# A fused attention and gated MoE kernel on one core: weight steps moved to VectorE, two chunks in turn, a rearranged start

## The chip, the cores and the metric

The kernel runs on one core of one Trainium2 chip. The metric is the device time of one execution in microseconds (us); lower is better. Engines are TensorE (PE; its weight loads PEld), VectorE (DVE), ScalarE (ACT), GpSimd (POOL) and SyncE (SP, which here only issues transfers; ScalarE issues some too). TensorE's clock has two levels, 1.2 and 2.4 GHz; the profile gives the granted clock as a fraction of the higher one.

## What is computed

```python
# attention: q, k, v are [4, 8, 576, 64]; hidden layer of 32
scores = matmul(q, k^T) / sqrt(64)
x      = log1p(|i - j|) / log1p(max(i, 1))             # [576, 576]
scores = scores + (relu(x * w1 + b1) @ w2) per head     # the position bias
attn   = softmax(scores) ;  y = attn @ v                # -> 2304 tokens x 512
# gated MoE layer: 512 -> 1536 -> 512
out = (sigmoid(y @ w_gate) * (y @ w_val)) @ w_out
```

The MoE weights arrive as 64-bit floats.

## The kernel before

The kernel has three parts, one after the other on the same engines.

**The bias (0 to about 107 us).** Nine chunks of 64 rows. For each hidden unit the relu is a switch that is on or off; the switches of a chunk (16 groups) are 0/1 tiles `ind` and `far`, and TensorE sums them with the coefficients `cfs` into PSUM tiles `bps`. Most switches (`OWN`, 12 groups) come from a matmul `y` of a position table `lt` with prepared weights `wy`, which ScalarE (a steep sigmoid) or, for the groups in `OWN_DVE`, VectorE (a comparison) turns into `ind`; `y` lies in two PSUM buffers. The four others (`far`) come from comparing a distance table `dist` with an `edge`, worked out by `edges()`: some scalars per hidden unit, an Exp over `pos` on ScalarE, then VectorE passes. For chunk 0 all this stands ahead of the first sums, with the loads of the small weights (`wr`, `pk`, `wb`, `w2r`, in 15 transfers on the queues of SP and ScalarE) and of `pos`, `dist` and `xt`, SP's in the order of the code. From chunk 1 on, the switches of the next chunk are made between the sums of this one. Single steps of the attention's preparation are started in between by `begun()`.

**The attention (about 107 to 376 us).** 16 units (a head pair and a batch), 9 steps each: scores, bias and row minimum (VectorE, `en`), Exp (ScalarE), transposes, products with v. q and k of unit u + 1 are prepared while unit u runs: `prep_q` is a ScalarE copy `part` in step 1; `raw` has one buffer for q and one for k, so a load waits until the unit before has been prepared. The stage's order is written out by hand.

**The MoE (from about 376 us).** 2304 tokens in six chunks of T = 384 (A, B, then the rest, called C0 onwards here), 12 blocks f of 128 hidden units. A step (c, f) makes 24 matmuls of gates (`pg`, then `pu`) and, in TensorE's order after the gates of the next step, 9 matmuls of outputs (`po`); in between ScalarE makes `g` = sigmoid, VectorE `g` = `pu` * `g`, ScalarE `gh`, VectorE `gl` (`gated`). A matmul in full precision takes each weight as a high and a low part. Chunks A and B are run interleaved as ORDER says; from then on, f by f.

The 36 weight blocks (f, z), z = gate, val, out, are converted during A and B. The first six were narrowed during the bias part; the other 30 pass `narrow`: size (ScalarE, L175), clamp (L178), low (L181), top (L184), tail (L187), then `upper` (ScalarE, L822) and `lower` (L827, hi/lo difference). `CLENG` and `LOENG` name the engine of the clamp and of `lower`. One call of `convert()` begins a block and moves each block under way by one step, in the order of the code on each engine: the `lower` of one block, low, top and tail of the next, the clamp of the one after. An A step makes two such calls, one ahead of `gated` and one after it, a B step one, and where the next gates' weights are not ready, calls are made at once until they are.

During the steps of B, the four parts of x for chunk C0 are loaded and prepared as `XNEXT` says: ("l", n) and ("r", n) load, ("p", n) prepares (VectorE add and product, ScalarE `xhi`, VectorE `xlo`). C0's x takes the buffer of A's x, so a ("p", n) must stand after A11's gates. The outputs of a finished chunk leave through ScalarE copies `ob` (two buffers) and stores.

Of the kernel before, what the change touches and what calls it, by code (L numbers as in the profile page):

```python
# [19 lines left out]
HID = 32  # L20
# [29 lines left out]
PLAN = {  # L50
# [39 lines left out]


def const_tables():
# [16 lines left out]
    pick = np.zeros((4, 32, 15), np.float32)  # L109
    for i in range(27):  # L110
        pick[:, i, ROWS[i // 4][1] if i < 24 else i - 24] = 1.0
        pick[:, i, 3:7] = np.eye(4, dtype=np.float32)[i % 4] if i < 24 else 0.0
        pick[:, i, 7:11] = 0.0 if i < 24 else 1.0
    for r in range(4):
        pick[r, :, 11 + r] = 1.0
# [3 lines left out]
    return {"steps": np.repeat(steps, 32, axis=0).astype(np.float16), "lpos": np.ascontiguousarray(lpos), "xtab": xtab,  # L119
            "lx": lx.reshape(NCH, 128, len(OWN) // 4, S), "pick": pick.reshape(128, 15)}  # L120


@with_exitstack
def tile_kernel(ctx, tc, q, k, v, w1, b1, w2, w_gate, w_val, w_out, steps, lpos, xtab, lx, pick, out, phases="0AB"):
    nc = tc.nc
# [6 lines left out]
    with ExitStack() as right, ExitStack() as att:  # L132
# [58 lines left out]

def bias(tc, w1, b1, w2, steps, lpos, xtab, lx, pick, biases, biasL, moe, begun):

# [5 lines left out]
    with ExitStack() as ph:  # L199
# [42 lines left out]
        for i in range(WARM):  # L242
            nc.tensor.matmul(out=ps[:, i % 2], lhsT=warm[:, 0:128], rhs=warm, start=True, stop=True)
        for z, (o, col) in enumerate(((wl, 3), (wt, 7))):
            nc.vector.tensor_tensor(
                out=o, in0=wr[:, z].rearrange("p (o m) -> p o m", o=1).to_broadcast([128, 4, HID]),
                in1=pk[:, col:col + 4].rearrange("p (g o) -> p g o", o=1).to_broadcast([128, 4, HID]), op=ALU.mult)
        nc.vector.tensor_tensor(out=wl, in0=wl, in1=wt, op=ALU.add)
        for part in range(3):
            nc.vector.tensor_copy(out=wh, in_=wl)  # L250
            if part == 0:
                nc.vector.tensor_scalar(out=wt, in0=wh, scalar1=pk[:, 0:1], scalar2=None, op0=ALU.mult)
            else:
                nc.vector.scalar_tensor_tensor(out=wt, in0=wh, scalar=pk[:, part:part + 1], in1=wt, op0=ALU.mult, op1=ALU.add)
            if part < 2:
                nc.vector.tensor_tensor(out=wl, in0=wl, in1=wh, op=ALU.subtract)
        for r in range(4):
            nc.vector.tensor_scalar(
                out=wy[:, r], in0=wt.rearrange("p g m -> p (g m)"), scalar1=pk[:, 11 + r:12 + r], scalar2=None, op0=ALU.mult)
        cf = cp.tile([128, 2, H, 4], F32, name="cf")  # L260
        nc.gpsimd.memset(cf, 0.0)
        for g in range(4):
            r = slice(32 * g, 32 * g + 32)
            for ab in range(2):
                nc.gpsimd.tensor_scalar(out=cf[r, ab, :, g], in0=w2r[r], scalar1=wb[r, ab:ab + 1], scalar2=8.0, op0=ALU.mult, op1=ALU.mult)
        conv = moe.narrow_ahead(pool("cvw", 2), pool("cvm", 2))

        def edges():
# [89 lines left out]

        edges()
# [46 lines left out]
def attention(tc, att, q, k, v, biases, biasL, ident, xs, rs, extra):  # L406
# [277 lines left out]
class Moe:  # L684
# [202 lines left out]
    def run(self):  # L887
# [5 lines left out]
        with ExitStack() as ph, tc.manual_schedule():  # L893
# [6 lines left out]
            for i, cf in enumerate(order + [None]):  # L900
# [65 lines left out]
```

## Time and profile before

| | us |
|---|---|
| median of 3 runs (lowest to highest) | 850.3 (849.32 to 852.1) |
| the profiled execution | 854.13 |
| its span | 852.2 |
| TensorE busy in the span | 804.8 |
| VectorE, ScalarE, GpSimd busy | 522.1, 428.8, 335.1 |

The span is the time from the first to the last instruction of the profiled execution; its own time holds a little more. Busy time is an average over parts with different limits, so it has to be read part by part.

### The profile page before, as it was taken

How to read it: one execution, taken by the hardware profiler on the slowest of the kernel's cores; microseconds unless marked ns; L12 is line 12 of the kernel's file. 1: busy time of each engine (PE TensorE's matmuls, PEld its weight loads, DVE VectorE, ACT ScalarE, POOL GpSimd, SP SyncE). 2: the span in 40 equal slices, each digit the busy share in tenths (PEclk: the TensorE clock that was granted, in tenths of full speed). 3: DMA queues.
4: the chain of work that ended last, by engine and by line, in shares of the span. 5: the costliest groups of instructions: out<-in, count | busy, mean ns of one | idle time of the engine just before them, and what ended most of it. 6: DMA issues, size and time to landing. Idle time of an engine off the chain costs nothing.

```text
span 852.2 us, 16999 instructions
## 1 busy us (share of the span) xinstructions
PE 804.8 (94%) x6500; PEld 749.6 (88%) x6500; DVE 522.1 (61%) x1059; ACT 428.8 (50%) x912; POOL 335.1 (39%) x360
## 2 busy tenths in 40 slices
PE   4999989999999999888999979999999999999998
PEld 1788879999999998878899858999999999999997
DVE  5588878999889989986888894311412331141211
ACT  2788859989899897754444433211221221122112
POOL 1233469999899979751456661000000000000000
PEclk7899999999999999999999999999999999999999
DMA  4433144656646586559612202030120103011000
GB/s 140 133 130 101 64 122 109 182 150 168 173 125 182 148 213 184 167 163 331 207 62 83 88 1 82 21 112 1 38 88 24 34 5 111 1 38 38 1 1 37
DMA packets 51999, 86.41 MB, mean 101 GB/s; under 512 B 6480, under 2 KB 28112, under 8 KB 51920
## 3 DMA queue, kind: packets, MB, share of 16 engines
q1 hardware_dynamic: 49568, 82.45, 33.0%
q10 hardware_dynamic: 2352, 2.90, 1.0%
q8 instruction: 51, 0.84, 0.4%
q14 instruction: 28, 0.23, 0.1%
HBM read 60.08 MB, written 15.80 MB: 89 GB/s over the span
## 4 chain that ended last, share of the span: by engine, by line
PE 65%; DVE 16%; ACT 5%; DMA 5%; issue 5%; POOL 3%; SPq 1%; ACTq 0%; DVEq 0%; POOLq 0%
PE po L876 13%; PE pu L855 13%; PE pg L855 13%; PE sc L538 7%; PE acc L618 7%; PE pt L561 6%; DVE wm L184 5%; PE bps L330 2%; PE y L306 2%; ACT ind L311 2%; DVE wm L181 2%; PE pt L581 1%; DMA xin<-xs 1%; DVE btmp L338 1%; DVE g L864 1%
## 5 line engine op out<-in xcount | busy, mean ns | idle before, releaser
L855 PE MATMUL pg<-xhi,w 128*128 128x384 f32 x576 | 160.6, 339 | 7.8 <-ACT g L863 6.7
L864 DVE TENSOR_TENSOR g<-pu,g 128x384 f32<-128x384 f32 x72 | 40.0, 556 | 206.0 <-PE pu L855 201.2
L855 PE MATMUL pu<-xhi,w 128*128 128x384 f32 x576 | 161.1, 340 | 5.1 <-POOL w L827 2.7
L876 PE MATMUL po<-w,gh 128*128 128x512 f32 x432 | 134.6, 393 | 0.0
L545 ACT ACTIVATE en<-en,mn 128x576 f32<-128x576 f32 x144 | 111.6, 775 | 31.8 <-DVE mn L542 30.8
L865 ACT ACTIVATE gh<-g 128x384 fp32r<-128x384 f32 x72 | 37.8, 525 | 158.9 <-DVE g L864 158.9
L855 PEld LDWEIGHTS pg<-xhi,w 128*128 128x128 f32 x576 | 105.4, 189 | 13.3 <-ACT g L863 8.9
L538 PE MATMUL sc<-k,QS 128*128 128x288 f32 x640 | 112.8, 302 | 1.7 <-DVE bias L346 0.6
L855 PEld LDWEIGHTS pu<-xhi,w 128*128 128x128 f32 x576 | 105.7, 189 | 8.6 <-POOL w L827 3.7
L542 DVE CUSTOM_DVE_ANT_0 en<-sc,bias 128x576 f32<-128x576 f32 x128 | 93.8, 751 | 7.2 <-PE sc L538 6.1
L855 PE MATMUL pu<-xlo,w 128*128 128x384 f32 x288 | 97.1, 337 | 0.0
L855 PE MATMUL pg<-xlo,w 128*128 128x384 f32 x288 | 97.0, 337 | 0.0
L538 PEld LDWEIGHTS sc<-k,QS 128*128 128x128 f32 x640 | 92.6, 190 | 3.2 <-DVE mn L542 1.0
L561 PE MATMUL pt<-ident,en 128*128 128x128 f32 x576 | 88.0, 276 | 4.1 <-DVE aL L461 1.9
L876 PEld LDWEIGHTS po<-w,gh 128*128 128x128 f32 x432 | 80.7, 189 | 12.2
L863 ACT ACTIVATE g<-pg 128x384 f32<-128x384 f32 x72 | 35.1, 487 | 108.3 <-PE pg L855 108.3
L618 PE MATMUL acc<-aH,vv 128*128 128x288 f32 x256 | 81.6, 335 | 6.2 <-DVE xe L621 3.5
L876 PE MATMUL po<-w,gl 128*128 128x512 f32 x216 | 84.5, 391 | 0.0
L561 PEld LDWEIGHTS pt<-ident,en 128*128 128x128 f32 x576 | 69.3, 142 | 7.3 <-ACT en L545 3.4
L618 PE MATMUL acc<-aL,vv 128*128 128x288 f32 x256 | 71.9, 298 | 0.0
L311 ACT ACTIVATE ind<-y 128x576 bf16<-128x576 f32 x103 | 64.4, 657 | 13.6 <-PE y L306 11.5
L461 DVE TENSOR_TENSOR aL<-pt,aH 128x512 fp32r<-128x512 f32 (+1 forms) x112 | 66.7, 607 | 7.4 <-ACT aH L460 7.4
(113 smaller groups left out, 1506.1 us busy)
## 6 DMA issues: line engine op xcount, KB each, us to landing
kr<-in_k_dram SPq DMA_DIRECT2D x32, 288.0 KB
QS<-part SPq DMA_DIRECT2D x64, 144.0 KB, 2.6
xs<-xe SPq DMA_DIRECT2D x32, 288.0 KB, 3.5
xin<-xs SPq DMA_DIRECT2D x48, 192.0 KB, 3.3
vr<-in_v_dram SPq DMA_DIRECT2D x16, 320.0 KB, 3.5
qr<-in_q_dram SPq DMA_DIRECT2D x16, 288.0 KB
xrec<-rs SPq DMA_DIRECT2D x48, 96.0 KB, 4.0
ww<-in_moe_w_val_dram SPq DMA_DIRECT2D x9, 512.0 KB, 6.5
```

Of the source, the lines that this page charges most:

```text
L184: nc.vector.scalar_tensor_tensor(out=t, in0=hi, scalar=-0x40000000, in1=t, op0=ALU.bitwise_and, op1=ALU.bitwise_or)
L311: nc.scalar.activation(out=o, in_=y[:, :, 0:HF], func=AF.Sigmoid, scale=float(2.0 ** 64))
L461: return lambda: nc.vector.tensor_tensor(out=lo, in0=ps, in1=hi.bitcast(F32), op=ALU.subtract)
L538: nc.tensor.matmul(out=ps[:, e, 0:HF], lhsT=l, rhs=r[:, HF * e:HF * e + HF], start=(i == 0), stop=(i == len(mms) - 1))
L542: nc.vector.tensor_tensor_reduce(out=half(en), in0=ps[:, :, 0:HF], in1=half(nbias), scale=-0.125, scalar=3.0e38, op0=ALU.add, op1=ALU.min, ...
L545: nc.scalar.activation(out=en, in_=en, func=AF.Exp, bias=mn, scale=-1.0, accum_out=sm)
L561: nc.tensor.transpose(pt[:, J], en[:, 128 * J:128 * J + 128], ident)
L618: nc.tensor.matmul(out=acc[:, 0:HF], lhsT=l, rhs=r, start=(i == 0), stop=(i == len(mms) - 1))
L855: self.nc.tensor.matmul(out=(pg, pu)[z], lhsT=l, rhs=r, start=(kc == 0 and i == 0), stop=(kc == 3 and i == 2))
L864: nc.vector.tensor_tensor(out=g, in0=pu, in1=g, op=ALU.mult)
L865: nc.scalar.activation(out=gh, in_=g, func=AF.Copy)
L876: self.nc.tensor.matmul(out=po, lhsT=l[:, tt], rhs=r, start=(f == 0 and i == 0), stop=(f == self.NF - 1 and i == 2))
```

## The change

These things are changed together.

- `LOENG` and `CLENG`: every `lower` and every clamp of the weight conversion is done by VectorE.
- `ORDER`: B7 and B8 stand between A8, A9 and A10.
- `XAFTER`: the preparation of x for C0 moves to B9 (two parts), B10 and B11.
- The small weights are laid out on the host as one array `small` [128, 89], loaded by one transfer at the head of SP's queue; `pos` and `dist` are loaded by ScalarE's queue.
- An Exp of one element at the start (`early`).
- The scalars of `edges()` and the Exp over `pos` stand ahead of the weight steps; the passes over `pos`, `dist` and `edge` are two and one instead of four and one, with the constants folded, after the weight steps; `wy` is made by one instruction instead of four.
- `cf` is made by four GpSimd instructions on all partitions instead of a memset and eight.
- In chunk 0, half of the `y` tiles use the two buffers of `bps` (`SIDE`), VectorE makes four `ind` instead of five, and the three `far` instructions stand after groups 2, 4 and 6.
- `load_q(1)` is issued right after `spread_q(0)`, ahead of k's preparation and load.

```diff
+SIDE = (2, 3)
+OWN_DVE = (5, 9, 11, 13)
-OWN_DVE = (1, 3, 5, 9, 11)
-ORDER = "A0 A1 B0 A2 B1 A3 B2 A4 B3 A5 B4 A6 B5 A7 B6 A8 A9 A10 A11 B7 B8 B9 B10 B11"
+ORDER = "A0 A1 B0 A2 B1 A3 B2 A4 B3 A5 B4 A6 B5 A7 B6 A8 B7 A9 B8 A10 A11 B9 B10 B11"
+XAFTER = {5: (("l", 0), ("r", 0)), 6: (("l", 1),), 7: (("r", 1), ("l", 2)), 9: (("p", 0), ("p", 1), ("l", 3), ("r", 2)),
+          10: (("p", 2), ("r", 3)), 11: (("p", 3),)}
-LOENG = lambda nc, f, z: nc.vector if f == 0 else nc.gpsimd
-CLENG = lambda nc, f, z: nc.gpsimd if f > 4 and (f + z) % 2 else nc.vector
+LOENG = lambda nc, f, z: nc.vector
+CLENG = lambda nc, f, z: nc.vector
...
+        sm = cp.tile([128, 2 * HID + 17 + H], F32, name="small")
+        nc.sync.dma_start(out=sm, in_=small)
+        wr, pk = sm[:, 0:2 * HID].rearrange("p (z m) -> p z m", z=2), sm[:, 2 * HID:2 * HID + 15]
+        wb, w2r = sm[:, 2 * HID + 15:2 * HID + 17], sm[:, 2 * HID + 17:]
-        nc.sync.dma_start(out=wr[:, 0], in_=w1.to_broadcast([128, HID]))
-        nc.scalar.dma_start(out=wr[:, 1], in_=b1.rearrange("(o m) -> o m", o=1).to_broadcast([128, HID]))
-        nc.sync.dma_start(out=pk, in_=pick)
         lt = load_lx(0)
-        for g in range(4):
-            r = slice(32 * g, 32 * g + 32)
-            nc.sync.dma_start(out=wb[r, 0:1], in_=w1.rearrange("o m -> m o"))
-            nc.scalar.dma_start(out=wb[r, 1:2], in_=b1.rearrange("(m o) -> m o", o=1))
-            nc.sync.dma_start(out=w2r[r], in_=w2)
...
-        nc.sync.dma_start(out=pos, in_=lpos)
-        nc.sync.dma_start(out=dist, in_=steps)
+        nc.scalar.dma_start(out=pos, in_=lpos)
+        nc.scalar.dma_start(out=dist, in_=steps)
+        early = cp.tile([128, 1], F32, name="early")
+        nc.gpsimd.memset(early, 0.0)
+        nc.scalar.activation(out=early, in_=early, func=AF.Exp)
...
+        sgn, off = edges()          # the nine scalars and the Exp over pos, ahead of the weight steps
...
-        for r in range(4):
-            nc.vector.tensor_scalar(
-                out=wy[:, r], in0=wt.rearrange("p g m -> p (g m)"), scalar1=pk[:, 11 + r:12 + r], scalar2=None, op0=ALU.mult)
+        group = pk[:, 11:15]
+        nc.vector.tensor_tensor(
+            out=wy, in0=wt.rearrange("p (o g) m -> p o (g m)", o=1).to_broadcast([128, 4, 128]),
+            in1=group.rearrange("p (r o) -> p r o", o=1).to_broadcast([128, 4, 128]), op=ALU.mult)
+        half = float(2.0 ** 23 - 0.5)
+        nc.vector.tensor_scalar(out=pos, in0=pos, scalar1=1000.0, scalar2=half, op0=ALU.min, op1=ALU.add)
+        nc.vector.tensor_scalar(out=edge, in0=pos, scalar1=-half, scalar2=sgn, op0=ALU.add, op1=ALU.mult)
+        nc.vector.tensor_scalar(out=dist, in0=dist, scalar1=sgn, scalar2=off, op0=ALU.mult, op1=ALU.subtract)
...
-            v.tensor_scalar(out=dist, in0=dist, scalar1=sgn, scalar2=None, op0=ALU.mult)
-            v.tensor_scalar(out=pos, in0=pos, scalar1=1000.0, scalar2=None, op0=ALU.min)
-            v.tensor_scalar(out=pos, in0=pos, scalar1=float(2.0 ** 23 - 0.5), scalar2=None, op0=ALU.add)
-            v.tensor_scalar(out=pos, in0=pos, scalar1=float(0.5 - 2.0 ** 23), scalar2=None, op0=ALU.add)
-            v.tensor_scalar(out=edge, in0=pos, scalar1=sgn, scalar2=off, op0=ALU.mult, op1=ALU.add)
...
-                y = py.tile([128, 2, 512], F32, name="y")
+                if c == 0 and n % 4 in SIDE:
+                    y = pp.tile([128, 2, 2, H, 32], F32, name="bps").rearrange("p a b h j -> p a (b h j)")
+                else:
+                    y = py.tile([128, 2, 512], F32, name="y")
...
-            if far:
+            if far and i in (2, 4, 6):
                 far.pop(0)()
...
     spread_q(0, o)
+    load_q(1)
     yield
     prep_k(0, 0)
     yield
     prep_k(0, 1)
     yield
     load_k(1)
-    load_q(1)
...
-                    self.x_steps(c + 1, x, xin, xrec, XNEXT.get(f, ()))
+                    self.x_steps(c + 1, x, xin, xrec, (XNEXT if c > 1 else XAFTER).get(f, ()))
```

## Rows read from the trace of the kernel before

**Rows 1.** The page's chain that ended last, by engine, in shares of the span.

```profile
PE 65%; DVE 16%; ACT 5%; DMA 5%; issue 5%; POOL 3%; SPq 1%; ACTq 0%; DVEq 0%; POOLq 0%
```

**Rows 2.** The table of stages: the stretch in us from the span's start, its length, the busy time of PE, PEld, DVE, ACT and POOL with the count of instructions, the granted TensorE clock, the DMA engines' busy share and GB/s.

```profile
9.80:24.65 14.85, 6.89 (x28) 3.48 (x29) 9.77 (x30) 7.25 (x9) 1.20 (x4) 0.50 0.55 168
...
132.00:376.00 244.00, 235.92 (x1842) 230.99 (x1841) 221.34 (x526) 212.23 (x510) 212.94 (x231) 0.99 0.60 163
...
409.00:485.30 76.30, 75.62 (x393) 69.29 (x394) 67.84 (x90) 30.70 (x61) 44.41 (x27) 1.00 0.31 96
485.30:515.00 29.70, 21.49 (x96) 17.30 (x95) 26.70 (x32) 10.37 (x21) 18.06 (x11) 0.94 0.05 17
515.00:852.20 337.20, 333.63 (x1768) 313.25 (x1766) 85.64 (x156) 72.23 (x143) 1.29 (x1) 1.00 0.13 40
```

**Rows 3.** The chain in order of time, in the MoE after the conversion: start, length, what. The first `pg` piece of two steps that follow each other.

```profile
523.41 2.08 PE pg L855 x12
...
529.62 2.08 PE pg L855 x12
```

**Rows 4.** ScalarE's timeline: start, length, engine, line, operation, out<-in; in brackets the idle time before it and its releaser. The sigmoids of A1, A2, A8, A9, A10 and A11.

```profile
394.42 0.48 ACT L863 ACTIVATE g<-pg 128x384 f32<-128x384 f32 x1
...
408.57 0.47 ACT L863 ACTIVATE g<-pg 128x384 f32<-128x384 f32 x1
...
485.28 0.47 ACT L863 ACTIVATE g<-pg 128x384 f32<-128x384 f32 x1
...
496.93 0.51 ACT L863 ACTIVATE g<-pg 128x384 f32<-128x384 f32 x1
...
506.96 0.47 ACT L863 ACTIVATE g<-pg 128x384 f32<-128x384 f32 x1
...
514.92 0.47 ACT L863 ACTIVATE g<-pg 128x384 f32<-128x384 f32 x1
```

**Rows 5.** The timelines of VectorE (first two rows) and GpSimd (next row) just ahead of A10's sigmoid; and the groups of VectorE's instructions from 396 to 485 us for L184 and L187 (busy us, mean ns, idle before).

```profile
504.01 0.69 DVE L184 SCALAR_TENSOR_TENSOR wm<-ww,wm 128x512 int32<-128x512 int32 x1
504.74 1.65 DVE L187 SCALAR_TENSOR_TENSOR wm<-ww,wm 128x512 int32<-128x512 int32 x1
...
504.39 1.46 POOL L827 TENSOR_TENSOR w<-wm,w 128x512 fp32r<-128x512 f32 x1 [2.02 <-ACT w L822]
...
L184 DVE SCALAR_TENSOR_TENSOR wm<-ww,wm 128x512 int32<-128x512 int32 x21 | 33.3, 1588 | 0.7
L187 DVE SCALAR_TENSOR_TENSOR wm<-ww,wm 128x512 int32<-128x512 int32 x21 | 18.2, 867 | 0.7
```

**Rows 6.** VectorE's timeline: a `lower` on VectorE, one block's steps while GpSimd was idle, and a gated step from its `g` to the instruction after its `gl`.

```profile
378.96 0.68 DVE L827 TENSOR_TENSOR w<-ww,w 128x512 fp32r<-128x512 f32 x1
...
390.81 0.43 DVE L181 TENSOR_SCALAR wm<-wm 128x512 int32<-128x512 int32 x1
391.28 0.69 DVE L184 SCALAR_TENSOR_TENSOR wm<-ww,wm 128x512 int32<-128x512 int32 x1
392.00 0.69 DVE L187 SCALAR_TENSOR_TENSOR wm<-ww,wm 128x512 int32<-128x512 int32 x1
392.61 0.42 DVE L178 TENSOR_SCALAR wm<-wm 128x512 f32<-128x512 f32 x1
...
399.65 0.55 DVE L864 TENSOR_TENSOR g<-pu,g 128x384 f32<-128x384 f32 x1
...
401.27 0.42 DVE L181 TENSOR_SCALAR wm<-wm 128x512 int32<-128x512 int32 x1
```

**Rows 7.** ScalarE's timeline: the third output copy of chunk A.

```profile
525.27 0.60 ACT L884 ACTIVATE ob<-po 128x512 f32<-128x512 f32 x1 [1.72 <-DMA out_dram<-ob]
```

**Rows 8.** The chain in order of time through the start: start, length, what.

```profile
1.16 5.27 DMA wb<-in_b_dram
...
9.12 3.05 DMA pos<-in_lpos_dram
...
13.53 0.77 ACT pos L284
14.32 1.28 ACT L311
15.62 0.66 ACT ind L311
...
24.65 1.95 PE bps L330 x48
```

**Rows 9.** VectorE's timeline in the start: the first weight step, the four `wy` instructions, the first and the last scalar of `edges()`; and the tile view of `w2r`, the time of its transfers from issue to landing.

```profile
6.34 0.50 DVE L245 TENSOR_TENSOR btmp<-wr,pk 128x128 f32<-128x128 f32 x2 [6.34 <-DMA pk<-in_pick_dram]
...
9.48 0.87 DVE L258 TENSOR_SCALAR wy<-btmp,pk 128x128 bf16<-128x128 f32 x4
...
10.27 0.15 DVE L275 TENSOR_SCALAR et<-wb 128x1 f32<-128x1 f32 x1
...
11.30 0.16 DVE L283 TENSOR_TENSOR et<-et 128x1 f32<-128x1 f32 x1
...
DMA to landing us min/median/max: 1.5/1.5/1.5
```

**Rows 10.** The chain in order of time at the attention's first unit.

```profile
113.16 5.49 DMA qr<-in_q_dram
118.65 0.46 issue
```

More of the change, by code (lines that the diff above doesn't have):

```diff
@@ L71, in host_layout @@
     data["v"] = np.ascontiguousarray(v.transpose(0, 1, 4, 2, 3, 5))
+    w1, b1, w2 = data.pop("w1").reshape(1, HID), data.pop("b1").reshape(1, HID), data.pop("w2")
+    data = {**{n: data.pop(n) for n in "qkv"}, "small": np.ascontiguousarray(np.concatenate(
+        [np.repeat(w1, 128, 0), np.repeat(b1, 128, 0), picks(), np.tile(w1.T, (4, 1)), np.tile(b1.T, (4, 1)), np.tile(w2, (4, 1))],
+        axis=1)), **data}
     return {n: a.view(np.int64) if a.dtype == np.float64 else a for n, a in data.items()}
@@ L89, with picks @@
 ROWS = ((0, 0), (0, 1), (1, 0), (0, 2), (2, 0), (1, 1))
+def picks():
+    pick = np.zeros((4, 32, 15), np.float32)
+    for i in range(27):
+        pick[:, i, ROWS[i // 4][1] if i < 24 else i - 24] = 1.0
+        pick[:, i, 3:7] = np.eye(4, dtype=np.float32)[i % 4] if i < 24 else 0.0
+        pick[:, i, 7:11] = 0.0 if i < 24 else 1.0
+    for r in range(4):
+        pick[r, :, 11 + r] = 1.0
+    return pick.reshape(128, 15)
 def const_tables():
@@ L108, in const_tables @@
             lx[c, i % 4, 4 * t:4 * t + 4, i // 4] = turn(parts[x])
[L109 to L113, printed above, removed]
-    for r in range(4):
-        pick[r, :, 11 + r] = 1.0
     steps = np.abs(np.arange(2 * S)[None, :] - S - np.arange(4)[:, None]) + 1
@@ L119, in const_tables, with tile_kernel @@
     return {"steps": np.repeat(steps, 32, axis=0).astype(np.float16), "lpos": np.ascontiguousarray(lpos), "xtab": xtab,
-            "lx": lx.reshape(NCH, 128, len(OWN) // 4, S), "pick": pick.reshape(128, 15)}
+            "lx": lx.reshape(NCH, 128, len(OWN) // 4, S)}
 @with_exitstack
-def tile_kernel(ctx, tc, q, k, v, w1, b1, w2, w_gate, w_val, w_out, steps, lpos, xtab, lx, pick, out, phases="0AB"):
+def tile_kernel(ctx, tc, q, k, v, small, w_gate, w_val, w_out, steps, lpos, xtab, lx, out, phases="0AB"):
     nc = tc.nc
@@ L152, in tile_kernel @@
         with tc.manual_schedule():
-            bias(tc, w1, b1, w2, steps, lpos, xtab, lx, pick, biases, biasL, moe, lambda: next(attn))
+            bias(tc, small, steps, lpos, xtab, lx, biases, biasL, moe, lambda: next(attn))
         if "A" in phases:
@@ L189, in narrow, with bias @@
     return size, clamp, low, top, tail
-def bias(tc, w1, b1, w2, steps, lpos, xtab, lx, pick, biases, biasL, moe, begun):
+def bias(tc, small, steps, lpos, xtab, lx, biases, biasL, moe, begun):
     nc = tc.nc
@@ L243, in bias @@
             nc.tensor.matmul(out=ps[:, i % 2], lhsT=warm[:, 0:128], rhs=warm, start=True, stop=True)
[L244 to L257, printed above, removed]
-            nc.vector.tensor_scalar(
-                out=wy[:, r], in0=wt.rearrange("p g m -> p (g m)"), scalar1=pk[:, 11 + r:12 + r], scalar2=None, op0=ALU.mult)
[L260 to L266, printed above, removed]
         def edges():
@@ L284, in edges @@
             nc.scalar.activation(out=pos, in_=pos, func=AF.Exp, scale=ratio)
-            v.tensor_scalar(out=dist, in0=dist, scalar1=sgn, scalar2=None, op0=ALU.mult)
-            v.tensor_scalar(out=pos, in0=pos, scalar1=1000.0, scalar2=None, op0=ALU.min)
-            v.tensor_scalar(out=pos, in0=pos, scalar1=float(2.0 ** 23 - 0.5), scalar2=None, op0=ALU.add)
-            v.tensor_scalar(out=pos, in0=pos, scalar1=float(0.5 - 2.0 ** 23), scalar2=None, op0=ALU.add)
-            v.tensor_scalar(out=edge, in0=pos, scalar1=sgn, scalar2=off, op0=ALU.mult, op1=ALU.add)
+            return sgn, off
@@ new lines, in bias @@
+        sgn, off = edges()
+        for z, (o, col) in enumerate(((wl, 3), (wt, 7))):
+            nc.vector.tensor_tensor(
+                out=o, in0=wr[:, z].rearrange("p (o m) -> p o m", o=1).to_broadcast([128, 4, HID]),
+                in1=pk[:, col:col + 4].rearrange("p (g o) -> p g o", o=1).to_broadcast([128, 4, HID]), op=ALU.mult)
+        nc.vector.tensor_tensor(out=wl, in0=wl, in1=wt, op=ALU.add)
+        for part in range(3):
+            nc.vector.tensor_copy(out=wh, in_=wl)
+            if part == 0:
+                nc.vector.tensor_scalar(out=wt, in0=wh, scalar1=pk[:, 0:1], scalar2=None, op0=ALU.mult)
+            else:
+                nc.vector.scalar_tensor_tensor(out=wt, in0=wh, scalar=pk[:, part:part + 1], in1=wt, op0=ALU.mult, op1=ALU.add)
+            if part < 2:
+                nc.vector.tensor_tensor(out=wl, in0=wl, in1=wh, op=ALU.subtract)
@@ new lines, in bias @@
+        group = pk[:, 11:15]
+        nc.vector.tensor_tensor(
+            out=wy, in0=wt.rearrange("p (o g) m -> p o (g m)", o=1).to_broadcast([128, 4, 128]),
[3 more added lines that the diff above has]
+        nc.vector.tensor_scalar(out=edge, in0=pos, scalar1=-half, scalar2=sgn, op0=ALU.add, op1=ALU.mult)
@@ new lines, in bias @@
+        nc.vector.tensor_scalar(out=dist, in0=dist, scalar1=sgn, scalar2=off, op0=ALU.mult, op1=ALU.subtract)
+        cf = cp.tile([128, 2, H, 4], F32, name="cf")
+        for ab in range(2):
+            nc.gpsimd.tensor_tensor(
+                out=cf[:, ab], in0=w2r.rearrange("p (h o) -> p h o", o=1).to_broadcast([128, H, 4]),
+                in1=group.rearrange("p (o g) -> p o g", o=1).to_broadcast([128, H, 4]), op=ALU.mult)
+            nc.gpsimd.tensor_scalar(out=cf[:, ab], in0=cf[:, ab], scalar1=wb[:, ab:ab + 1], scalar2=8.0, op0=ALU.mult, op1=ALU.mult)
@@ L291, in switches @@
+        conv = moe.narrow_ahead(pool("cvw", 2), pool("cvm", 2))
         def switches(c, lt):
@@ L302, in one @@
             def one(i):
-                y = py.tile([128, 2, 512], F32, name="y")
                 n = OWN.index(i)
+                if c == 0 and n % 4 in SIDE:
+                    y = pp.tile([128, 2, 2, H, 32], F32, name="bps").rearrange("p a b h j -> p a (b h j)")
+                else:
+                    y = py.tile([128, 2, 512], F32, name="y")
                 for e in range(2):
@@ L357, in leave @@
                         out=biasL[64 * e:64 * e + 64, :, j], in0=rest[r, 0, e::2], in1=tmp[r, 0, e::2], op=ALU.add)
-        edges()
         ind, own, far = switches(0, lt)
```

4 lines of the change are left out of this document (removed).

## The prediction

> **What bounds the kernel now.** I read the page's chain by engine first, then a table of the stages, then each stage's own chain. TensorE carries 65% of the chain that ends last, VectorE 16% [rows 1], and the stages have different limits. From 132 to 376 us (attention) and from 515 us to the end TensorE is busy 97 to 99% at full clock [rows 2]; nothing in the change shortens that work. One step of the MoE (24 gate matmuls, 9 output matmuls) takes 529.62 - 523.41 = 6.21 us when TensorE runs freely [rows 3]. So what can be won is the time in which TensorE is kept waiting. The table has two such places: 9.80 to 24.65 us (TensorE 6.89 of 14.85 us, granted clock 0.50, that is 1.2 GHz), and 485.3 to 515 us (21.49 of 29.70).
>
> The second place is measured best by the times at which ScalarE starts the sigmoid of each A step [rows 4]. A1 to A2: 14.15 us for two steps (12.42 when free). A2 to A8, six A/B pairs: 76.71, so 12.79 a pair against 12.42. A8 to A11, three A steps with no B between: 29.64 against 18.63. Together A2 to A11 takes 106.35 us for 15 steps, 13.2 more than 93.15. VectorE sets this pace: it is busy 67.84 of 76.30 us in the pairs and 26.70 of 29.70 after [rows 2], and most of what is left is the wait for ScalarE's `gh` between `g` and `gl`.
>
> **Weight steps on VectorE.** Each of 30 blocks passes L181, L184, L187 and the clamp L178 on VectorE, some clamps and nearly all `lo` subtractions (L827) on GpSimd. The rows show what that does: L184, started at 504.01 while GpSimd is idle, takes 0.69 us; GpSimd's L827 starts at 504.39, and the L187 that starts next, at 504.74, takes 1.65, where one alone takes 0.69 [rows 5, 6]. In most blocks it is L184 that is hit; its mean in the pairs is 1.59 [rows 5]. So each GpSimd `lo` costs VectorE about 0.96 us. Alone, the start-to-start times are 0.47 (L181), 0.72 (L184), 0.61 (L187), plus 0.42 for the clamp; a `lo` that VectorE already does takes 0.68, as long as L187, so I count 0.61 to the next start for it too [rows 6]. One block wholly on VectorE is 0.47 + 0.72 + 0.61 + 0.42 + 0.61 = 2.83 us. A gated step holds VectorE 1.62 (399.65 to 401.27, wait for `gh` included) [rows 6]. A pair converts three blocks: 2 x 1.62 + 3 x 2.83 = 11.73 us, below TensorE's 12.42. The bounds of a block's cost: 2.83, and 3.18, which is today's (12.79 - 3.24) / 3; I take 2.83, because no GpSimd instruction is left in the stage. Both bounds leave the pairs near TensorE's pace.
>
> Why VectorE's order does no harm: in an A step two blocks stand ahead of `g`, so that `g` comes 7.28 us after the previous one where TensorE needs 6.21; it is about 1 us late, but the next matmuls into `pu` start 4.1 us after the gates (outputs 2.05, `pg` 2.08), and the B step, with one block, wins it back. A `lo` of the second gate block comes about 0.5 + 1.62 + 0.61 = 2.7 us after the B gates, wanted at 4.1.
>
> **Chunks in turn.** The new order has A11 at place 20 instead of 18; B7 and B8 stand between A8, A9 and A10, so each of those pairs has three blocks for two steps. Only A10, A11 remain next to each other. There the `lo` of A11's first block comes 0.5 + 1 + 1.62 + 0.61 = 3.7 us after A10's gates where TensorE asks at 2.05: 1.65 us, and the second block about 0.3 more. I take a stall of 1.9 (bounds 0 and 5.4, the latter A8 to A9's stall today). A2 to A11 then is 17 steps: 17 x 6.21 + 1.9 = 107.5. Before, the same steps took 106.35 plus two B steps later, 118.8. Gain 11.3. A1 to A2 has three blocks in a row on VectorE, each about 0.5 shorter; of its 1.73 us stall I give 1.0 back. The stage ahead (376 to 394 us) is paced by weight transfers; three `lo` more on VectorE there sit beside those waits: 0, bounds -1 and +1.8 (three `lo`).
>
> **x of chunk 2 later.** It must write where chunk 0's x lies, so it follows A11: two parts after B9, one after B10, one after B11, directly before chunk 2's first gates. In B9 ScalarE also copies chunk 0's outputs; the third copy waits 1.72 for a store [rows 7]. That puts the two `xhi` behind it, B10's sigmoid behind them (about 0.5 us past TensorE's need), and the last part's `xhi` and `xlo`, about 3.9 and 4.4 us after B11's gates, meet a need at 3.6. I charge 1.3 (bounds 0 and 3). MoE in all: -11.3 - 1.0 + 1.3 = -11.0.
>
> **The start.** Today the first `ind` waits for `pos`: SP's queue sits behind `wb` (5.27 us), issues six more small transfers, and issues `pos` at 9.12; it lands 3.05 later, then come a table load, the Exp (0.77), another load (1.28), and ScalarE's first `ind` at 15.62; the sums start at 24.65 [rows 8]. After: one small transfer issued first (0.72). Its landing t0 lies between 1.5 us (the 1 KB `w2r` [rows 9]) and 5.27 (the `wb` row) after issue: 2.2 to 6.0. The nearest case, the small `pk` among the very first transfers, which releases VectorE at 6.34 [rows 9], went second in its queue, so I take 5.4, just under. On VectorE the edge scalars come first (10.27 to 11.46, 1.2 us), then the weight steps (6.34 to 10.35, 4.0, with one `wy` pass for four, about 0.15 less): `wy` at t0 + 5.05 = 10.4 [rows 9]. `pos`, issued at once on ScalarE's queue, is there by about 6; Exp and sigmoid table are done by about 8.5, under cover of that VectorE work. Then 12 `y` tiles: TensorE 6.9 at half clock (its busy time in the stretch [rows 2]), ScalarE 8 x 0.66 = 5.3, VectorE about 7 of the 9.77 it does now (edge scalars gone ahead, one `ind` and two passes fewer); with four PSUM buffers instead of two these overlap. Sums start at about 10.4 + 7.0 = 17.4: gain 7.2. Bounds: t0 at 6.0 and 1.6 us of imperfect overlap give 5.0; t0 at 2.2 gives 10.4. `xt`, issued some 8 us earlier, still lands before the first sums leave. The bias stage after it (VectorE, ScalarE, TensorE in turns) has no wait on an absolute time in its chain, so it moves as a whole. `cf`'s eight small GpSimd instructions become four: 0, under the `y`s.
>
> The rows put a small landing anywhere from 1.5 to 5.3 us after issue. The Trainium skill (DMA: Bandwidth & Descriptors, Latency and other measured facts) gives a DMA a fixed cost of about 2 us; by that t0 would be an estimated 2.7 and the start would gain about 9.9. The `w2r` row agrees with it, the first transfers of this trace do not.
>
> **q ahead of k.** SP's load of q for unit 1 stands behind k's, which waits for GpSimd; it lands at 118.65 and ScalarE starts `part` at 119.10 after 0.46 us [rows 10]. Put right behind `spread_q` it is there in time; k's loads are not later, since they wait for GpSimd, not for the queue. What ends last next is `en`, waiting for VectorE. Gain 0.5, bounds 0 and 1.0.
>
> **Sum.** -7.2 - 0.5 - 11.0 = -18.7. The profiled execution took 854.1 us (span 852.2, 1.9 around it) and would become 835.4; the runs' median is 850.3, so **831.6 us**.
>
> **Rivals.** (a) The move between engines gives nothing: VectorE pays for its new work what the lost stretches return, and a pair stays at 12.79. Then 8.5 x 12.79 + 1.9 = 110.6 against 118.8, MoE -8.2 + 1.3 = -6.9, total -14.6: 835.7. Against it stand the 0.68 and 0.69 rows; for it, that VectorE is the busy engine. The Trainium skill (Perfetto Trace Analysis, Optimizing Scalar/DVE Operations) warns that moving operations between these two engines might not help, since they share a port; the stretched rows agree on the sharing.
> (b) Slower: the 1.65 us is not GpSimd's doing, and L184 and L187 keep their means in the pairs, 1.59 and 0.87 [rows 5]. A block then costs 0.47 + 1.62 + 0.90 + 0.42 + 0.61 = 4.02 us, a pair 15.3; 8.5 x 15.3 = 130 against 118.8: +11.2 + 1.3 - 7.7 = +4.8, 855.1. It decides from 3.83 us a block. Against it: 504.01 and 504.74, where the stretch moves to the other line with GpSimd's start.
> (c) The start's gain is halved, the small transfer late or the `y`s still in lockstep: 835.2.
> (d) Attention swallows the earlier start, at a transfer that isn't ready sooner: 838.8. Its loads are ordered by engines, not by the clock, which speaks against.
> (e) No stall at A11 or for x, and t0 near 4: 826.
>
> **Chances.** Forecast 56% (827 to 835); (a) 15%, (c) 11%, (d) 7%, (e) 7%, (b) 4%. The range 824.5 to 839 leaves out (b) and the far ends of (d), (e) and the forecast's own bounds. 0.3% (2.6 us) is about what this measurement can tell from no change: faster 0.95, same 0.01, slower 0.04.
>
> **What would show it.** Right: the sums start near 17 us; L184 and L187 at 0.69 throughout, GpSimd silent after 376; A-to-A sigmoid distances of 12.4 through A10, one gap of about 2 us before A11, a small one before chunk 2's first gates. Wrong: L184 still near 1.6; pairs at 12.8; sums starting after 20; a TensorE gap of several us at the first gates of chunk 2; an `en` in unit 0 waiting for a transfer.

## The result and the profile after

The changed kernel takes **825.27 us** (median of four executions, 821.78 to 826.03), beside 849.84 for the kernel before on the same chip (849.32 to 852.1): ratio 0.9698, 95% interval 0.9665 to 0.9731. In a later session it was 824.82 against 851.43, ratio 0.9688 (0.9660 to 0.9716). The direction and the forecast's places were right; the gain is 24.6 to 26.6 us where 18.7 were forecast, so the time lies below the forecast's own 827 to 835 us, at the lower edge of the wider range.

The profiled execution took 826.03 us, its span is 823.9. The chain by engine, which answers [rows 1]:

```profile
PE 78%; DVE 10%; ACT 5%; DMA 4%; issue 2%; POOL 0%; SPq 0%; POOLq 0%; ACTq 0%; DVEq 0%
```

TensorE carries 78% of it instead of 65%; GpSimd is gone from it. The table of stages, with the columns of [rows 2]:

```profile
7.99:13.42 5.43, 4.23 (x24) 2.33 (x25) 5.36 (x15) 4.62 (x8) 0.00 (x0) 1.00 0.49 136
...
392.00:465.13 73.13, 73.13 (x391) 68.88 (x390) 60.87 (x116) 33.81 (x61) 0.00 (x0) 1.00 0.34 106
465.13:490.00 24.87, 24.87 (x134) 23.41 (x133) 20.25 (x39) 11.07 (x21) 0.00 (x0) 1.00 0.14 43
490.00:523.00 33.00, 31.91 (x166) 29.00 (x165) 16.83 (x31) 9.47 (x19) 0.00 (x0) 1.00 0.14 48
```

Both places at which TensorE was kept waiting are nearly closed. The `y` stage lasts 5.43 us, with VectorE busy 5.36 of it; from 392 to 490 us TensorE is never idle and VectorE has slack (60.87 of 73.13); what is left of the second place is 1.09 us of idle time in 490 to 523. The start on VectorE's timeline (first `et`, the `wy` pass) and TensorE's (first `y`, first sums), beside [rows 8, 9]:

```profile
3.14 0.15 DVE L259 TENSOR_SCALAR et<-small 128x1 f32<-128x1 f32 x1 [3.14 <-DMA small<-in_small_dram]
...
7.38 0.69 DVE L286 TENSOR_TENSOR wy<-btmp,small 128x512 bf16<-128x512 f32 x1
```

```profile
8.12 0.67 PE L319 MATMUL y<-lt,wy 128*128 128x288 bf16 x4 [1.65 <-DVE wy L286]
...
13.42 0.69 PE L343 MATMUL bps<-cfs,ind 128*128 128x64 bf16 x18
```

`small`, issued at 0.73, releases VectorE at 3.14, and the sums start at 13.42. In [rows 8] the chain enters them at 24.65; on TensorE's timeline of before the first of them starts at 24.45, which is the number used below. ScalarE's sigmoids of A2, A8, A9, A10, A11 and chunk 2's first step (the chunk called C0 above), beside [rows 4]:

```profile
392.29 0.48 ACT L875 ACTIVATE g<-pg 128x384 f32<-128x384 f32 x1
...
465.13 0.48 ACT L875 ACTIVATE g<-pg 128x384 f32<-128x384 f32 x1
...
477.57 0.47 ACT L875 ACTIVATE g<-pg 128x384 f32<-128x384 f32 x1
...
489.01 0.47 ACT L875 ACTIVATE g<-pg 128x384 f32<-128x384 f32 x1
496.08 0.47 ACT L875 ACTIVATE g<-pg 128x384 f32<-128x384 f32 x1
...
521.62 0.49 ACT L875 ACTIVATE g<-pg 128x384 f32<-128x384 f32 x1 [1.36 <-PE pg L867]
```

A8 to A9 is now one pair, 12.44 us; A10 to A11 are 7.07 us apart. The groups of VectorE's weight steps from 396 to 485 us, beside [rows 5], and TensorE's waits from 490 to 523 us:

```profile
L197 DVE SCALAR_TENSOR_TENSOR wm<-ww,wm 128x512 int32<-128x512 int32 x22 | 15.2, 692 | 0.8
L200 DVE SCALAR_TENSOR_TENSOR wm<-ww,wm 128x512 int32<-128x512 int32 x22 | 15.2, 692 | 0.7
L839 DVE TENSOR_TENSOR w<-wm,w 128x512 fp32r<-128x512 f32 x22 | 15.0, 684 | 0.0
```

```profile
PE pg L867 <- DVE w L839: 0.9, 1, 0.9
```

L197 and L200 are the lines that were L184 and L187. Their means fell from 1588 and 867 ns to 692 both.

**Where the time went.** Both kernels were profiled twice (runs e8 and e13 below are the second time). Cut at four marks, the profiles differ like this (us; first pair, second pair):

| stretch | forecast | first pair | second pair |
|---|---|---|---|
| start to the first sums | -7.2 | 24.45 to 13.42: -11.03 | 24.39 to 13.72: -10.67 |
| first sums to the first `acc` matmul | -0.5 | 108.84 to 107.80: -1.04 | 109.14 to 107.65: -1.49 |
| first `acc` to A2's sigmoid | -1.0 | 275.28 to 271.07: -4.21 | 274.83 to 271.76: -3.07 |
| A2's sigmoid to the end | -10.0 | 443.63 to 431.61: -12.02 | 443.64 to 431.57: -12.07 |
| span | -18.7 | -28.3 | -27.3 |

The first and the last line repeat to 0.4 us. The third does not: eight profiles of kernels whose code is the changed kernel's between these marks gave 269.5 to 274.0, and e7 below, whose code is that of the kernel before up to A8, gave 272.53, where the two profiles of before have 275.28 and 274.83. The profiled executions differ by 28.1 and 27.0 us, the medians by 24.6 and 26.6: both profiled executions of before, 854.13 and 853.86 us, lie above their sessions' medians (850.3 and 851.29), those of after, 826.03 and 826.87, less so (825.27 and 824.82).

### The profile page after: what moved, and what is told of

Read it like the earlier page. It is cut to its first block, busy times and chain, and to the rows that moved or that the text cites. A ratio compares the mean times of both kernels' runs of the same rounds, so it can differ in the third digit from the quotient of the medians.

```text
span 823.9 us, 16933 instructions
## 1 busy us (share of the span) xinstructions
PE 793.3 (96%) x6500; PEld 743.0 (90%) x6500; DVE 506.3 (61%) x1097; ACT 431.6 (52%) x914; POOL 261.3 (32%) x312
## 4 chain that ended last, share of the span: by engine, by line
PE 78%; DVE 10%; ACT 5%; DMA 4%; issue 2%; POOL 0%; SPq 0%; POOLq 0%; ACTq 0%; DVEq 0%
PE pu L867 17%; PE pg L867 17%; PE po L888 17%; PE sc L550 7%; PE acc L630 7%; PE pt L573 6%; PE bps L343 3%; DVE btmp L351 2%; PE y L319 2%; ACT ind L324 2%; DVE en L554 1%; DMA xin<-xs 1%; PE pt L593 1%; ACT en L557 1%; DVE bias L359 1%
## 5 line engine op out<-in xcount | busy, mean ns | idle before, releaser
L867 PE MATMUL pu<-xhi,w 128*128 128x384 f32 x576 | 159.0, 336 | 0.4 <-DVE w L839 0.4
L343 PE MATMUL bps<-cfs,ind 128*128 128x64 bf16 x1458 | 67.5, 193 | 2.8 <-DVE bias L359 2.2
```

Of the source, the lines that this page charges most:

```text
L343: nc.tensor.matmul(out=o, lhsT=st, rhs=cfs[:, part], start=(part == 0), stop=(part == 2))
L867: self.nc.tensor.matmul(out=(pg, pu)[z], lhsT=l, rhs=r, start=(kc == 0 and i == 0), stop=(kc == 3 and i == 2))
```

## The experiments

**e8 and e13: both kernels again.** No edit.

> The kernel before once more, for a second profile. If the 3 us by which the changed kernel is earlier still between 320 and 355 us, where nothing was changed, are the scatter of one execution, this profile is about 3 us shorter there than the first (first sigmoid of A0 near 383 instead of 386) and its span about 848 to 850; if they belong to the change, it repeats the first within 0.5 us.

> The changed kernel once more, beside the next run. Forecast from the runs so far: ratio to the kernel before 0.968 to 0.973; in its profile first acc to A2's sigmoid 269.5 to 274 us (five profiles of kernels that do not differ there gave 269.5 to 274.0), A2's sigmoid to the end of the span 431.6.

Measured: spans 852.0 and 824.7, the second pair of the table. In the second profile of before A0's sigmoid came 3.6 us earlier (382.34), as forecast for scatter, but A2's still at 408.36 (408.57), and the span did not shorten to the 848 to 850 us of that alternative. e13 fell within its forecast.

**e1 and e2: clock or buffers in the `y` stage.**

```
-WARM = 12
+WARM = 8        (e1)
-SIDE = (2, 3)
+SIDE = ()       (e2)
```

> The changed kernel with 8 warm-up matmuls instead of 12, so that TensorE idles about 3.3 us before its first y (as it did in the kernel before) instead of 1.65. Theory: the y stage came out at 5.43 us and not 7.0 because the short idle time left the granted clock at 1.00. Then here the clock is near 0.50 from about 8.5 us on, the y stage takes about 7.0, the sums start at about 15.0 and the time is 1.5 to 2.5 us above the changed kernel's. Rival: the four PSUM buffers alone make the stage short, since VectorE ends it; then the sums start within 0.5 us of 13.4 whatever the clock, and the time is within 0.6 us.

> The changed kernel with all y tiles in the two buffers of their own pool, as before, instead of four. Theory that the clock made the stage short: at full clock two buffers cost little, sums at 13.4 to 14.2, time 0 to 0.8 us more. Rival, the buffers: a y's round through TensorE (0.4), ScalarE (0.66) and the waits between them is about 1.6 us, two at a time, so 12 tiles take about 9 us instead of 5.4, the sums start near 17 and the time is 3 to 4 us more.

Measured: e1 827.0 us (ratio 0.9712, 0.9664 to 0.9761), e2 832.56 (0.9772, 0.9724 to 0.982). The forms of `y` (min/median/max ns) in the changed kernel and in e1, then the sums' start on TensorE's timeline in e1 and in e2:

```profile
L319 PE MATMUL y<-lt,wy x12: 282/283/297, 8.1 to 12.2; 128*128 128x288 bf16 x12
```

```profile
L319 PE MATMUL y<-lt,wy x12: 421/447/448, 8.4 to 13.0; 128*128 128x288 bf16 x12
```

```profile
14.45 0.69 PE L343 MATMUL bps<-cfs,ind 128*128 128x64 bf16 x18 [0.49 <-ACT ind L324]
```

```profile
16.38 1.17 PE L343 MATMUL bps<-cfs,ind 128*128 128x64 bf16 x18
```

e1's matmuls ran slow all through, four in 0.96 us, and yet the stage from the first `y` to the sums took 6.00 us (8.45 to 14.45) against 5.30: less than the theory's 7.0, more than the rival allowed. With two buffers it took 7.97 (8.41 to 16.38; granted clock 0.50, that is 1.2 GHz, from 10 us on). In the second profile of the changed kernel, e13, the clock fell with four buffers (its table of stages, and TensorE's timeline):

```profile
9.00:10.00 1.00, 1.00 (x6) 0.65 (x5) 1.00 (x4) 1.00 (x2) 0.00 (x0) 0.50 1.00 269
10.00:11.00 1.00, 1.00 (x6) 0.65 (x5) 0.97 (x4) 1.00 (x3) 0.00 (x0) 0.50 0.50 162
```

```profile
8.34 1.09 PE L319 MATMUL y<-lt,wy 128*128 128x288 bf16 x4 [2.37 <-DVE wy L286]
...
13.72 0.45 PE L343 MATMUL bps<-cfs,ind 128*128 128x64 bf16 x10
```

Half the clock for about 3 us, and the stage takes 5.38; in e4, at 0.50 throughout, it takes 6.20. So slow matmuls cost 0.1 us here, 0.7 to 0.9 where they are slow all through (e1, e4), and the buffers are worth more: with slow matmuls four take 6.0 to 6.2 us, two take 8.0. Two buffers at a granted clock of 1.00 were not run. e2 pays about what its rival said: the sums are 3.0 us later, the first `acc` 4.3 (part of its sums ran at half clock too). Its timed ratio is 0.007 worse, 6 us, with intervals wide enough for 4.3. e1's is 0.001 worse, 1.2 us, which the intervals do not tell from nothing; its sums are 1.0 later (0.3 of it from `small`), its first `acc` 2.0.

**e3, e4, e9: why `small` came at 3.1 and not 5.4.** All three add loads that nothing uses.

```
+for g in range(4):                                                  (e3, ahead of pos on ScalarE's queue)
+    nc.scalar.dma_start(out=wbx[32 * g:32 * g + 32, 0:1], in_=small[0:1, 0:HID].rearrange("o m -> m o"))
+nc.sync.dma_start(out=wrx, in_=small[0:1, 0:HID].to_broadcast([128, HID]))   (e4, ahead of small)
+nc.sync.dma_start(out=wrx, in_=small[:, 0:HID])                              (e9, ahead of small)
```

> The changed kernel with four loads of 32 x 4 bytes put ahead on ScalarE's queue, one element to a partition, as the kernel before had them; what they load is not used. Theory: such scattered elements hold up all other early transfers, which is why nothing released VectorE before 6.34 us in the kernel before. Then small lands near 5.5 to 6 us instead of 3.1, and wy is done near 10.5 to 11 instead of 8.07. Rival: a transfer on another queue does not touch it; small lands at 3.1 to 3.5.

> The changed kernel with one 16 KB load, the same 32 numbers to each of 128 partitions, issued ahead of small on SP's queue, as the kernel before had it; what it loads is not used. Theory of the prediction, that place two in the queue is what made the nearest row late: small lands near 5.4 instead of 3.1. Rival: a place in the queue costs only the issue, 0.4 us; small lands at 3.5 to 3.8.

> As the run with a 16 KB load ahead of small on SP's queue, but each partition reads 128 bytes of its own row instead of all reading the same 128 bytes. If the place in the queue made small late there (6.98 us): it lands near 7 here too. If the one source row read 128 times did: it lands at 3.1 to 3.8.

VectorE's first instruction in e3, e4 and e9, in this order, and ScalarE's Exp in e3:

```profile
2.73 0.15 DVE L262 TENSOR_SCALAR et<-small 128x1 f32<-128x1 f32 x1 [2.73 <-DMA small<-in_small_dram]
```

```profile
6.98 0.15 DVE L261 TENSOR_SCALAR et<-small 128x1 f32<-128x1 f32 x1 [6.98 <-DMA small<-in_small_dram]
```

```profile
4.07 0.15 DVE L261 TENSOR_SCALAR et<-small 128x1 f32<-128x1 f32 x1 [4.07 <-DMA small<-in_small_dram]
```

```profile
12.13 0.78 ACT L271 ACTIVATE pos<-pos,et 128x576 f32<-128x576 f32 x1 [6.20 <-DMA pos<-in_lpos_dram]
```

Second place costs about 1 us (4.07). Second place behind one source row read 128 times costs 3.8 (6.98), more than either forecast of e4, and such a load stood ahead of `pk` in the kernel before, whose row, 6.34 [rows 9], I had taken as nearest. 4-byte elements on the other queue do not touch `small` (2.73), but they hold what stands behind them: `pos`, issued at 2.66, arrives at 12.13, the sums start at 20.32, and the execution took 833.37 us (e4's 831.46, e9's 830.16; one execution each).

**e5, e6, e7: the MoE's parts on the kernel before.**

```
e5 = e6 + e7
e6: +LOENG = lambda nc, f, z: nc.vector        +CLENG = lambda nc, f, z: nc.vector
e7: +ORDER = "... A8 B7 A9 B8 A10 A11 B9 B10 B11"      +XAFTER = {...}, used for chunk 2
```

> The kernel before with the MoE's part of the change alone (weight steps on VectorE, the new order, x of chunk 2 after A11); start and q as before. By the prediction 11.0 us faster than before; by the two traces (first sigmoid to the end) 12.4. If the MoE's gain were lost without the earlier start, or part of the difference between the traces were noise of one execution: less than 10.

> The kernel before with clamps and lo subtractions on VectorE alone; order and x of chunk 2 as before. By the prediction's block of 2.83 us: 6 pairs x 0.37 = 2.2, A1 to A2 1.0, and three A steps in a row at 1.62 + 2 x 2.83 = 7.28 each, 21.84 instead of 29.64, 7.8: 11.0 us faster in all. Rival (a), the move gives nothing: within 1 us of before. Rival (b): some us slower.

> The kernel before with the new order and x of chunk 2 after A11; clamps and lo subtractions on the engines they had. By the prediction's rows: A2 to A10 is 8 pairs at 12.79 and A10 to A11 takes about 10.0 as A9 to A10 did, 112.3 instead of 118.8, and 1.3 back for x: 5.2 us faster. If the order were worth something only with the steps on VectorE: within 1 us of before.

| run | ratio (interval) | in us of 851.3 | A2's sigmoid to the end, against 443.6 |
|---|---|---|---|
| e5 both | 0.9860 (0.9825 to 0.9894) | -11.9 (-9.0 to -14.9) | -12.5 |
| e6 engines | 0.9933 (0.9910 to 0.9957) | -5.7 (-3.7 to -7.7) | -5.9 |
| e7 order | 0.9914 (0.9878 to 0.9951) | -7.3 (-4.2 to -10.4) | -8.6 |

The MoE's part is worth what was forecast for it (11.0 lies in e5's interval), and by the profiles as much without the earlier start (12.5) as with it (12.0). The halves were mis-forecast: e6 beyond its interval, e7 by its profile, 8.6 against 5.2, which its timed interval still holds. The groups of the two weight steps from 410 to 485 us in e6 and in e7 (there L186 and L189):

```profile
L184 DVE SCALAR_TENSOR_TENSOR wm<-ww,wm 128x512 int32<-128x512 int32 x19 | 13.2, 692 | 0.6
L187 DVE SCALAR_TENSOR_TENSOR wm<-ww,wm 128x512 int32<-128x512 int32 x19 | 13.1, 692 | 0.6
```

```profile
L186 DVE SCALAR_TENSOR_TENSOR wm<-ww,wm 128x512 int32<-128x512 int32 x18 | 28.2, 1566 | 0.6
L189 DVE SCALAR_TENSOR_TENSOR wm<-ww,wm 128x512 int32<-128x512 int32 x17 | 15.5, 909 | 0.6
```

The stretch follows GpSimd's work, not the order: rivals (a) and (b) both fall here. e6 gives less than 11 because I gave an A step two blocks; without a B step beside it, it takes three (gate, value and output weights). VectorE's timeline in e6, A9 to A10 (sigmoids at 487.79 and 496.62):

```profile
490.84 0.68 DVE L827 TENSOR_TENSOR w<-wm,w 128x512 fp32r<-128x512 f32 x1
493.57 0.68 DVE L827 TENSOR_TENSOR w<-wm,w 128x512 fp32r<-128x512 f32 x1
496.30 0.69 DVE L827 TENSOR_TENSOR w<-wm,w 128x512 fp32r<-128x512 f32 x1
```

A block every 2.73 us (the prediction's sum for one was 2.83), three to a step of 8.83, so A8 to A11 still takes 25.69 there, not 21.84. The order cures that by itself: in e7 the same three steps with B7 and B8 between them take 32.76 for five. Of the 3.4 us that e7's profile gains beyond the forecast 5.2, 2.2 come from A10 to A11, which takes 7.85, as A10 to A11 did before ([rows 4]: 7.96), not the 10.0 of A9 to A10 that I used. Both parts cure the same three steps, and so the halves (14.5 by the profiles) exceed the whole (12.5).

**e10, e11, e12, e14: what could still be had.**

```
e10: cfs[:, part] = cf; cf -= cfs[:, part]  on nc.gpsimd behind cf, instead of nc.vector among the y
e11: START[0] "... X0 s w0 w4 ... X1 L3 s X2 X1 X1"  ->  "... X0 s s w0 w4 ... X1 L3 X2 X1 X1"
e12: e11, and two of START[1]'s "s" moved into START[0], behind "R2 X1" and "w2 X1"
e14: e10 and e12
```

> The changed kernel with the five small instructions that split cf into cfs on GpSimd, ahead of the y stage, instead of VectorE inside it. VectorE was busy 5.36 of the stage's 5.43 us and these five take about 1.0 of it; theory, VectorE ends the stage: sums 0.5 to 1.0 us earlier (12.4 to 12.9). Rival, TensorE's and ScalarE's turns end it: sums within 0.2 of 13.4.

> The changed kernel with one weight transfer (the gate weights of f = 2) issued on ScalarE's queue right behind the one before it, 360.5 us instead of 363.9, where it stood behind a ScalarE copy that waits for a transfer. Theory: A0's sigmoid stands behind the Abs of these weights (369.49), so it comes 2 to 3 us earlier, and A2 1 to 3 us. Rival: the DMA engines are full there; A2's sigmoid within 1 us of the changed kernel's, measured from the first acc matmul (271.1).

> As the run before it, with two more of the weight transfers (behind A0's sigmoid on ScalarE's queue so far) issued ahead of it. Theory: the stage from 360 to 392 us is short of transfers in flight in its first half; first acc to A2 falls by 2 to 5 us from 271.1. Rival, DMA engines full or a slot not yet free: within 1 us, or later if ScalarE stands before a slot.

> The changed kernel with cfs split on GpSimd ahead of the y stage and three weight transfers issued earlier. If the stage from 360 to 392 us waits for transfers that could have been in flight earlier: 2 to 4 us faster than the changed kernel, nearly all of it between first acc and A2's sigmoid (near 268.5). Rival, the 2.6 us of the single look was scatter of one execution: within 1 us of the changed kernel.

e10: first `y` to sums 5.03 instead of 5.30, but `small` came 0.33 later and the sums started at 13.49; the execution took 826.19 us. That is the rival's number, sums within 0.2 of 13.4: freed of 1 us of work, VectorE no longer ends the stage, and TensorE waits for ScalarE ahead of the sums:

```profile
13.49 0.70 PE L348 MATMUL bps<-cfs,ind 128*128 128x64 bf16 x18 [0.35 <-ACT ind L329]
```

e14, with the same edit and the clock at 0.50 from 9 to 11 us, took 5.43 for the stage, against e13's 5.38. e11 and e12 took 824.76 and 823.38 us, one execution each. The stages from 360 to 376 us in the changed kernel and in e12 (the DMA share is the last number but one):

```profile
360.00:376.00 16.00, 12.99 (x78) 12.27 (x77) 11.44 (x24) 5.39 (x11) 0.00 (x1) 1.00 0.83 272
```

```profile
360.00:376.00 16.00, 13.06 (x74) 11.84 (x72) 10.32 (x22) 5.74 (x11) 0.00 (x0) 1.00 1.02 315
```

The transfers did move forward (0.83 to 1.02; 0.95 in e14), and first `acc` to A2 took 269.69 us in e11, 268.45 in e12 and 269.37 in e14, the low end of the eight or just below it. In e11 A0's sigmoid no longer stands behind the Abs of those weights, but waits for TensorE's `acc` instead; from the first `acc` it came 0.4 us earlier (248.42 against 248.83), not 2 to 3. Timed, e14 gives 824.23 us, ratio 0.9673 (0.9646 to 0.9700), beside e13's 824.82, 0.9688 (0.9660 to 0.9716): 0.6 us, inside both intervals. That is the rival's "within 1 us" by the medians; whether it beats the changed kernel stays open.

## Why the prediction was right or wrong

**The landing of `small`: wrong by 2.3 us.** The step was "the nearest case, the small `pk` ..., went second in its queue, so I take 5.4". The row was near in size and time but not in what stood ahead of it. It landed at 3.1 to 3.5 in the runs that left the queues alone (issued at 0.73, there at 3.11 in the first). The Trainium skill's fixed cost of about 2 us (DMA: Bandwidth & Descriptors, Latency and other measured facts), which I had set aside for the rows, agrees with the measured 2.38 us.

**The `y` stage: wrong by 1.6.** Both large terms of "about 10.4 + 7.0" were too big. VectorE's "about 7 of the 9.77" came to 5.36 us: the profile's chain stays on VectorE from 8.07 to 12.96, but its fourth `ind` starts at 13.53, behind the sums' start. "TensorE 6.9 at half clock" was the busy time of 28 matmuls that came in pairs with waits between them (0.64 us for two at half clock), and the first profile has the clock at 1.00. Back to back and slow all through, the 24 need 0.24 us each, 5.8 in all (e1), and the stage is 0.7 to 0.9 longer (e1, e4). The overlap that I forecast for four buffers held. From VectorE's release to `wy` I had 5.05; it took 4.93 (3.14 to 8.07). Together the sums start 4.0 earlier than the forecast 17.4; against the starting point 24.45 that is 11.03 gained instead of 7.2.

**q ahead of k: right.** `part` moved by 12.04 (119.10 [rows 10] to 107.06), the bias stage ahead of it by 11.49: 0.55, forecast 0.5. No run has this edit alone. The rest of the table's second line is the first 48 sums, 1.57 us at full clock instead of 1.95.

**The block's cost: right.** 2.73 measured, 2.83 forecast; 692 ns where GpSimd is silent. The pairs run at TensorE's pace, 12.41 to 12.44 us from A4 to A9, as forecast. The Trainium skill's doubt that moving work between these two engines helps (Perfetto Trace Analysis, Optimizing Scalar/DVE Operations) isn't borne out in this direction: taken back to VectorE alone, the work gives 5.7 us (e6), because GpSimd's instruction had stretched VectorE's.

**The stalls: wrong by 1.1 together, and their base by 1.6.** On TensorE a step runs from its first gate matmul to that of the next step, 6.21 us when free. The first gate matmul of the step after A2 and of the step after A11, in the kernel before:

```profile
409.09 0.45 PE L855 MATMUL pg<-xhi,w 128*128 128x384 f32 x1 [1.44 <-ACT g L863]
...
517.02 0.34 PE L855 MATMUL pg<-xhi,w 128*128 128x384 f32 x1
```

The same two in the changed kernel, between them the first of A11 and its wait, and behind them the first of chunk 2's first two steps; then VectorE's `g` of A10 and the `lo` that A11 waits for:

```profile
392.93 0.34 PE L867 MATMUL pg<-xhi,w 128*128 128x384 f32 x1
...
492.34 0.33 PE L867 MATMUL pg<-xhi,w 128*128 128x384 f32 x1
...
493.77 0.62 PE L867 MATMUL pg<-xhi,w 128*128 128x384 f32 x2 [0.93 <-DVE w L839]
...
500.07 0.34 PE L867 MATMUL pg<-xhi,w 128*128 128x384 f32 x1
...
518.71 0.33 PE L867 MATMUL pg<-xhi,w 128*128 128x384 f32 x1
...
525.50 0.34 PE L867 MATMUL pg<-xhi,w 128*128 128x384 f32 x1
```

```profile
491.42 0.55 DVE L876 TENSOR_TENSOR g<-pu,g 128x384 f32<-128x384 f32 x1
...
493.04 0.68 DVE L839 TENSOR_TENSOR w<-wm,w 128x512 fp32r<-128x512 f32 x1
```

Before, these 15 steps took 107.93 us, 14.8 more than free. The failed term is "13.2 more than 93.15": it was taken between sigmoids, and A2's stands 0.5 us ahead of the next step's gates, A11's 2.1. After, the 17 steps take 107.14, 1.6 more than free (forecast 1.9), 1.5 of it in A11's step (7.73). There the mechanism was right: A10's gates are done at 490.29, VectorE's `g` comes 1.1 us later, its `lo` 3.4 us after the gates (forecast 3.7), and TensorE, which could run two matmuls without it, asks at 2.4 instead of 2.05. For x of chunk 2 1.3 was forecast; its first step takes 6.79, 0.6 over: B10's late sigmoid cost TensorE nothing. So the line is 14.8 - 1.6 - 0.6 = 12.6 instead of 10.0; the profiles have 12.0, because the rest of the run, behind chunk 2's first step, is 0.5 us longer (298.40 against 297.88), for which I know no reason.

**The mark at A2.** TensorE was busy without a gap from 392 us, yet the first two pairs measure 11.43 and 11.72 between sigmoids: these came ever closer behind its gates. The mark itself holds, as A2's sigmoid stands 0.5 us ahead of the next gates before and 0.6 after. Sigmoid distances are a sound measure only between sigmoids that stand alike to TensorE's steps.

**First `acc` to A2: open.** 1.0 forecast, 3 to 4 in the profiles, in a stage that scatters by 4.5. The medians leave 24.6 - 11.0 - 1.0 - 12.0 = 0.6 us for it with the first pair's numbers and 26.6 - 10.7 - 1.5 - 12.1 = 2.3 with the second's, so most of the excess may be the profiled executions of before. The profiles allow that: with e7, the code of before spans 272.5 to 275.3 there and overlaps the changed kernel's 269.5 to 274.0, and e5 and e6, which have the weight steps on VectorE but the old start, gave 272.7 and 272.1. It is argued, not shown.

**The rivals.** (e), "No stall at A11 or for x, and t0 near 4: 826", is nearest in time and had 7%, but that is partly luck: its terms add up to 827.0, the stalls were 2.1 together and not nothing, t0 was 3.1, and the `y` stage's 1.6 and the base's 1.6 are not in it. (a) fell by e6, (b) by the 692 ns, (c) by 13.42, and (d) by the first `acc`, 12.07 us earlier. The forecast took the middle or the cautious end of its bounds for t0, the stage and the stalls, and all came out faster, t0 and the stage by most.

## What to carry to other kernels

When a transfer's landing is estimated from a row, look at what stood ahead of it in its queue, not at its size: here the same small load lands 2.0 to 2.8 us after its issue when first, 2.9 behind an ordinary one and 5.8 behind a broadcast of one row. Busy time of an engine that works in turns with others is not the time it needs back to back; divide a gap-free run's length by its count instead. When two edits cure the same wait, forecast each alone as well: by the profiles the halves here, 5.9 and 8.6 us, make 12.5, not 14.5.

## What the runs showed of the hardware

- The granted clock in the `y` stage differs between executions of the same code: 1.00 throughout in the first profile (TensorE idle 1.65 us before the first `y`), 0.50 (1.2 GHz) from 9 to 11 us in the second (idle 2.37), with 0.08 us more for the stage. In e10 (idle 1.68) it stayed at 1.00, in e9 (idle 2.27) it was 0.50 from 11 to 13 us.
- The clock row can miss a slow engine: in e1 it reads 1.00 all through the stage, while the `y` matmuls took 447 ns, as in e13 at 0.50, instead of 283. There only 8 warm-up matmuls ran ahead, in 3.60 us.
- One 128-byte row broadcast to 128 partitions, first in its queue, delayed the next transfer by 2.9 us more than a plain load of the same size did (6.98 against 4.07). In e4 all transfers together moved at most 64 GB/s in any 0.2 us until 3.2 us; in e9 it was 102 GB/s and more from 1.8 us on.
